# Phase parts of an S4D and GLU kernel stored as blocks of 14 rows, each phase tile loaded by two transfers

## The chip, the cores and the metric

The kernel runs on one NeuronCore of a Trainium2 chip. The metric is the device time of one execution in microseconds (us), of which the median of several runs counts. Beside the times there is one profiled execution of the kernel, with a record of each instruction and transfer.

The engines are named as in the profile: PE is TensorE (its weight loads are PEld), DVE is VectorE, ACT is ScalarE, POOL is GpSimd, and SP is the engine that here only issues transfers. ACT and POOL issue transfers of their own as well. Each engine takes its instructions in a fixed order; an instruction that waits holds all that stand behind it on the same engine.

## The reference

The input x (2048 tokens, 448 channels) is normalised over its channels. Two branches take the result: a state space convolution (S4D) whose kernel of length 2048 is the sum of 256 complex exponentials per channel, applied by FFT, and a gated MLP (GLU) of width 1792. The output is the sum of x and both branches.

```python
def _A_ref(u, log_A_real, A_imag, C_real, C_imag, log_dt, D_skip):
    dt = jnp.exp(log_dt)
    A = -jnp.exp(log_A_real) + 1j * A_imag
    C = (C_real + 1j * C_imag) * dt[:, None]
    P = jnp.exp((A * dt[:, None])[:, :, None] * pos[None, None, :])
    K = 2.0 * jnp.einsum("dn,dnl->dl", C, P).real
    ...
    y = jnp.fft.irfft(Uf * Kf[None, :, :], L2)[:, :, :L]
    return y + u * D_skip[None, None, :]

def _B_ref(x, w_gate, w_up, w_down):
    g = jnp.einsum("bsd,df->bsf", x, w_gate)
    u = jnp.einsum("bsd,df->bsf", x, w_up)
    return jnp.einsum("bsf,fd->bsd", _sigmoid(g) * u, w_down)

xn = _layernorm(x, axis=-1)
return x + _A_ref(xn, ...) + _B_ref(xn, ...)
```

## The kernel before

Two Python generators, conv for the S4D branch and glu for the GLU branch, yield in turns, and a table of weights decides which goes next. So the program text interleaves the two. A scheduler with a cost model of its own then sets the order on each engine from that text, from priorities (hp) and from hints that one instruction is to be issued after another (issue_after). A small edit can so shift many rows.

The GLU works in float32 split into a high and a low part: gate (L693) makes three products per weight tile and x tile into the PSUM tile gu, then ACT's th (L701), DVE's hf (L704), ACT's hh (L709) and DVE's hl (L711). The down products po (L806) collect into acc by DVE (L811). gu and po share four PSUM buffers. Weights are loaded by SP into one buffer, wraw (w_load, L626 and L628, six transfers), then cast into wh by ACT (L743), with the rest in wl by DVE (L747). The second weight of all is loaded into raw1 at the start and cast as wh_268. In the first half of the GLU most weight parts are also stored to memory for later (wt_d L750, dt_d L773).

The S4D branch has four stages. First x is normalised and transposed, and its spectrum's first step is taken (x_spec). Second, prep computes for two halves h of 224 channels the magnitudes and the phases of the exponentials. Each phase has three values, U, V and T, and each is split into a high part (L388, ACT) and a low part (L393, POOL); these six parts per channel are stored to ph_d in memory by SP (L389, L394), one transfer of 112 partitions by 2 by 256 numbers for a part and a half, twelve in all. Third, kgen goes over 56 steps of 8 channels: PE turns the stored parts into angles by a product with a table sel (tr, L526), ACT makes sines and cosines S (L532 to L535), POOL makes powers of the magnitudes me and mf (L504), DVE multiplies both into Et and Ft (L586 to L588), and PE's ko (L600) sums over the states. Fourth, spectra multiplies spectra and transforms back (sp L888, pv L915).

A phase tile ph0 or ph1 holds 16 channels, two sets of eight. Partitions 32g to 32g+11 hold six parts of two channels; 32g+12 and 32g+13 hold ones; 32g+14 to 32g+25 hold the same twelve rows again, which sel multiplies with the other sign. The ones meet a large constant in sel, plus and minus, so that the sum is rounded to whole turns between. phase_load (L470 to L476) fills a tile by eight transfers of 12 partitions, four groups g at two places; the ones are set once by POOL (L468). The tiles are used in turn, and a tile is loaded anew as soon as PE has read it the second time, two tiles ahead:

```python
def phase_load(b):
    t = pht[b % 2]
    src = ph_d[16 * b : 16 * b + 16].rearrange("(k g e) i n -> g (e i) k n", k=2, g=4)
    for at in (0, 14):
        for g in range(4):
            r0 = 32 * g + at
            nc.sync.dma_start(t[r0 : r0 + 12].bitcast(F32), src[g])
```

Of the kernel before, what the change touches and what calls it, by code (L numbers as in the profile page):

```python
# [11 lines left out]
F32 = mybir.dt.float32  # L12
# [8 lines left out]
D = 448  # L21
N = 256
# [5 lines left out]
MAGIC = 1.5 * 2.0**23  # L28
# [27 lines left out]
def _tables():  # L56
# [15 lines left out]
    b = np.arange(NB)[:, None]  # L72
# [36 lines left out]
    for e in range(DC):  # L109
        g, r = e // 2, 6 * (e % 2)  # L110
        for at, sg in ((r, 1.0), (r + 14, -1.0)):
            sel[g, at : at + 2, 0, e] = sg * st
            sel[g, at + 2 : at + 4, 1, e] = sg * st
            sel[g, at + 4 : at + 6, 1, e] = sg
        sel[g, 12, :, e] = MAGIC
        sel[g, 13, :, e] = -MAGIC
    f = lambda v, s: np.ascontiguousarray(v.reshape(s).astype(np.float32))
# [7 lines left out]
        "c_sel": f(sel, (128, 512)),  # L125
        "c_id": np.eye(128, dtype=np.float32),
    }


@with_exitstack  # L130
def s4d_glu_kernel(ctx, tc, io):
    nc = tc.nc
# [7 lines left out]
    acc_d = dram.tile([128, 8, D], F32, name="acc_d")  # L140
    ph_d = dram.tile([D, 6, N], F32, name="ph_d")
    x1_d = dram.tile([64, NB, D], F32, name="x1_d")
# [193 lines left out]
    def prep(pool, h, srcs):  # L336
# [47 lines left out]
        rows = ph_d[2 * CP * h : 2 * CP * h + 2 * CP].rearrange("(t p) i n -> p t i n", t=2)  # L384

        def high(i, src):
            hi = slots[f"P{i}"][:, h]
            nc.scalar.copy(hi, src)  # L388
            nc.sync.dma_start(rows[:, :, 2 * i], three(hi).bitcast(F32))  # L389

        def low(i, src):
            lo = src.bitcast(F32R)
            nc.gpsimd.tensor_tensor(lo, src, slots[f"P{i}"][:, h], ALU.subtract)  # L393
            nc.sync.dma_start(rows[:, :, 2 * i + 1], three(lo).bitcast(F32))  # L394

# [49 lines left out]
    def kgen(pk):  # L445
# [24 lines left out]
        def phase_load(b):  # L470
            t = pht[b % 2]
            src = ph_d[16 * b : 16 * b + 16].rearrange("(k g e) i n -> g (e i) k n", k=2, g=4)
            for at in (0, 14):
                for g in range(4):
                    r0 = 32 * g + at
                    nc.sync.dma_start(t[r0 : r0 + 12].bitcast(F32), src[g])  # L476

# [528 lines left out]
    def conv():  # L1006
        with tc.tile_pool(name="psk", bufs=1, space=PSUM) as ps_, tc.tile_pool(
# [9 lines left out]
            with tc.tile_pool(name="pst", bufs=1, side="right", reuse_waits="tile") as pst:  # L1017
# [33 lines left out]
                nc.gpsimd.tensor_copy(sel[:, 0:1], zs[:, 7:8])  # L1051
                nc.gpsimd.dma_start(sel, io["c_sel"])
                nc.sync.dma_start(wk, io["c_wk"])
                nc.sync.dma_start(wx, io["c_wx"])
# [88 lines left out]
```

## Time and profile before

| quantity | value |
| --- | --- |
| median of 3 runs | 740.25 us (738.54 to 742.46) |
| the profiled execution's own time | 735.94 us |
| its span, first to last instruction | 734.2 us |
| mean granted TensorE clock | 0.978 of full speed |
| bytes moved by the DMA engines | 117.24 MB, mean 160 GB/s |
| SP's transfers (q1) | 91.87 MB, 45.3% of 16 engines' span |
| POOL's transfers (q0) | 5.90 MB, 3.0% of 16 engines' span |

A row of the timeline has its start in us, its length in us, engine, line, operation and what it writes and reads; in brackets stands the idle time ahead of it and what ended that. A row of the chain has start, length and what the chain went through there. A row of waits has in total the us, the times and the longest. PE stands for the matrix products as recorded; their ends are modelled.

### The profile page before, as it was taken

The numbers are of one execution on the slowest core, as the hardware profiler recorded it, in microseconds if no ns is written. First come the engines' busy times: TensorE is split into PE (matmuls) and PEld (weight loads), VectorE is DVE, ScalarE is ACT, GpSimd is POOL, SyncE is SP. The second block draws the span as 40 slices with busy tenths as digits, with TensorE's granted clock in tenths as the row PEclk, the third lists the DMA queues.
The fourth block names the chain that finished last, engine by engine and source line by source line (L and its number), as shares of the span: only waits on it lengthen the run. The fifth ranks groups of instructions, "written<-read, shape, count | busy, mean of one in ns | idle before, by whom it ended". The sixth has DMA issues, their size and how long they took to land.

```text
span 734.2 us, 19242 instructions
## 1 busy us (share of the span) xinstructions
PE 682.4 (93%) x7780; PEld 532.7 (73%) x7780; DVE 557.0 (76%) x776; ACT 421.1 (57%) x650; POOL 355.9 (48%) x423
## 2 busy tenths in 40 slices
PE   2898998999999899999999999998999999999995
PEld 2666787877877687565888877887877778776784
DVE  5899995699978989768667987977975555565543
ACT  3646483578677868797487787677652222323320
POOL 2110055684975986548467498486855001441002
PEclk9999999999999999699999999999999999999998
DMA  9946445444324635345972332332158999999845
GB/s 208 225 131 179 113 135 176 134 138 168 96 89 135 221 86 155 98 127 174 278 191 88 111 108 80 100 104 80 45 163 272 257 253 241 266 262 221 199 118 160
DMA packets 102984, 117.24 MB, mean 160 GB/s; under 512 B 13232, under 2 KB 90864, under 8 KB 102896
## 3 DMA queue, kind: packets, MB, share of 16 engines
q1 hardware_dynamic: 78736, 91.87, 45.3%
q10 hardware_dynamic: 21584, 18.24, 9.6%
q0 software_dynamic: 2576, 5.90, 3.0%
q8 instruction: 61, 1.00, 0.6%
q14 instruction: 27, 0.22, 0.1%
HBM read 72.13 MB, written 43.84 MB: 158 GB/s over the span
## 4 chain that ended last, share of the span: by engine, by line
PE 55%; DVE 17%; ACT 8%; DMA 8%; issue 5%; POOL 4%; SPq 2%; ACTq 1%; DVEq 0%; POOLq 0%
PE gu L693 23%; PE po L806 13%; PE sp L888 5%; PE ko L600 5%; PE pv L915 3%; PE tr L526 3%; DVE Ft L588 2%; DVE Et L587 2%; ACT S L535 2%; DVE Et L586 2%; DVE pm L440 2%; ACT S L532 1%; DMA sx<-x_d 1%; ACT S L533 1%; DMA tb<-in_c_tab_dram 1%
## 5 line engine op out<-in xcount | busy, mean ns | idle before, releaser
L504 POOL TENSOR_TENSOR me<-me,pm 128x32 f32<-128x32 f32 (+1 forms) x168 | 137.5, 819 | 114.8 <-DVE Et L587 102.9
L504 POOL TENSOR_TENSOR mf<-mf,pm 128x64 f32<-128x64 f32 (+1 forms) x112 | 113.8, 1016 | 5.2
L693 PE MATMUL gu<-xh,wh 128*128 128x512 f32 x336 | 100.2, 404 | 2.6 <-DVE acc L811 1.1
L693 PE MATMUL gu<-xh,wl 128*128 128x512 f32 x336 | 97.8, 396 | 0.0
L693 PE MATMUL gu<-xl,wh 128*128 128x512 f32 x336 | 96.2, 394 | 0.0
L586 DVE TENSOR_TENSOR Et<-me,S 128x1024 f32<-128x1024 f32 x56 | 80.1, 1430 | 18.1 <-ACT S L535 17.0
L587 DVE TENSOR_TENSOR Et<-me,S 128x1024 f32<-128x1024 f32 x56 | 78.9, 1410 | 15.4 <-ACT me L517 12.0
L806 PE MATMUL po<-dh,hh 128*128 128x448 f32 x224 | 85.1, 380 | 3.7 <-DVE acc L811 3.0
L588 DVE TENSOR_TENSOR Ft<-mf,S 128x1024 f32<-128x1024 f32 x56 | 79.3, 1416 | 5.5 <-ACT S L535 4.5
L806 PE MATMUL po<-dl,hh 128*128 128x448 f32 x224 | 83.2, 371 | 0.0
L806 PE MATMUL po<-dh,hl 128*128 128x448 f32 x224 | 82.4, 369 | 0.0
L693 PEld LDWEIGHTS gu<-xh,wh 128*128 128x128 f32 x336 | 61.2, 190 | 23.5 <-issue 6.1
L600 PEld LDWEIGHTS ko<-Et,Ft 128*32 128x32 f32 x3584 | 54.5, 111 | 32.3 <-DVE Ft L588 13.8
L532 ACT ACTIVATE S<-tr 128x1024 f32<-128x1024 f32 x56 | 57.7, 1030 | 33.2 <-PE tr L526 31.5
L600 PE MATMUL ko<-Et,Ft 128*32 128x64 f32 x3584 | 64.9, 223 | 12.4 <-DVE Ft L588 12.4
L693 PEld LDWEIGHTS gu<-xh,wl 128*128 128x128 f32 x336 | 63.7, 190 | 14.7 <-DVE ys L257 0.7
L693 PEld LDWEIGHTS gu<-xl,wh 128*128 128x128 f32 x336 | 63.8, 190 | 14.3 <-issue 0.7
L709 ACT CAST hh<-hf 128x512 fp32r<-128x512 f32 x56 | 34.9, 623 | 62.7 <-DVE hf L704 62.6
L704 DVE SCALAR_TENSOR_TENSOR hf<-th,gu 128x512 f32<-128x512 f32 x56 | 38.2, 682 | 40.4 <-PE gu L693 34.7
L701 ACT ACTIVATE th<-gu 128x512 f32<-128x512 f32 x56 | 33.6, 601 | 59.6 <-PE gu L693 46.1
L535 ACT ACTIVATE S<-S,hpi 128x1024 f32<-128x1024 f32 x56 | 65.6, 1172 | 0.0
L811 DVE SCALAR_TENSOR_TENSOR acc<-po,acc 128x448 f32<-128x448 f32 x80 | 48.1, 617 | 19.4 <-PE po L806 19.4
(198 smaller groups left out, 1295.1 us busy)
## 6 DMA issues: line engine op xcount, KB each, us to landing
sk_d<-sk ACTq DMA_DIRECT2D x14, 512.0 KB
sx<-x_d SPq DMA_DIRECT2D x32, 224.0 KB
skl<-sk_d SPq DMA_DIRECT2D x16, 448.0 KB
vp<-v_d SPq DMA_DIRECT2D x16, 448.0 KB
v_d<-vt SPq DMA_DIRECT2D x62, 112.0 KB
ph<-ph_d SPq DMA_DIRECT2D x224, 24.0 KB
wt_d<-wh SPq DMA_DIRECT2D x9, 512.0 KB
wt_d<-wl SPq DMA_DIRECT2D x9, 512.0 KB
```

Source lines behind the costliest of these rows:

```text
L504: ins = nc.gpsimd.tensor_tensor(m[:, :, w + a : 2 * w : n], m[:, :, a:w:n], par(base + i).unsqueeze(2).to_broadcast([128, 4 * DC, w // n]) ...
L532: nc.scalar.activation(rows(cs), pv, AF.Abs)
L535: sins[:] = [nc.scalar.activation(cs, cs, AF.Sin, scale=-TWO_PI, bias=hpi)]
L586: v.tensor_tensor(Et[:, :, :, 32:64], two(me[:, :, 32:64]), S[:, 1::-1], ALU.mult)
L587: v.tensor_tensor(Et[:, :, :, 0:32], two(me[:, :, 0:32]), S[:, 1:3, :, ::-1], ALU.mult)
L588: fts[:] = [v.tensor_tensor(Ft, two(mf), S[:, 3:5], ALU.mult)]
L600: mm = nc.tensor.matmul(ko[32 * j : 32 * j + 32, sl], Ft[:, cc, DC * h + 4 * q + j], Et[:, cc, DC * h + 4 * q + j], start=(k == 0), stop=( ...
L693: glu_mm[:] = [nc.tensor.matmul(ps, a_, b_, start=(n == 0), stop=(n == len(mm) - 1))]
L704: marks[1] = v.scalar_tensor_tensor(hf, th, 1.0, pgu[1], ALU.add, ALU.mult)
L806: glu_mm[:] = [nc.tensor.matmul(po, a_[:, bs], w_, start=(n == 0), stop=(n == 3 * fc - 1))]
L811: v.scalar_tensor_tensor(acc[:, b], po, 0.5, acc[:, b], ALU.mult, ALU.add)
L888: mm = nc.tensor.matmul(to, tb[:kk, t, 64 * c : 64 * c + 64], rhs, start=True, stop=True, skip_group_check=True,)
```

## The change

In memory each channel now has a block of 14 rows: six parts, two rows of ones, and the six parts again. So four channels are 56 rows that follow each other both in memory and in the tile, and a tile is loaded by two transfers of 56 partitions, at partitions 4 to 59 and 68 to 123. sel has its rows moved to match. Every part is stored twice (store, 24 transfers for 12), and the ones are copied into ph_d once from a new constant input, by POOL's queue. Line numbers move by two to six.

```diff
     for e in range(DC):
-        g, r = e // 2, 6 * (e % 2)
-        for at, sg in ((r, 1.0), (r + 14, -1.0)):
+        g = e // 2
+        r = 4 * (1 - g % 2) + 14 * (e % 2)
+        for at, sg in ((r, 1.0), (r + 8, -1.0)):
             sel[g, at : at + 2, 0, e] = sg * st
             sel[g, at + 2 : at + 4, 1, e] = sg * st
             sel[g, at + 4 : at + 6, 1, e] = sg
-        sel[g, 12, :, e] = MAGIC
-        sel[g, 13, :, e] = -MAGIC
+        sel[g, r + 6, :, e] = MAGIC
+        sel[g, r + 7, :, e] = -MAGIC
...
+        "c_one": np.ones((D, 2, N), np.float32),
...
-    ph_d = dram.tile([D, 6, N], F32, name="ph_d")
+    ph_d = dram.tile([D, 14, N], F32, name="ph_d")
...
+        def store(i, src):
+            for at in (i, i + 8):
+                nc.sync.dma_start(rows[:, :, at], src)
+
         def high(i, src):
             hi = slots[f"P{i}"][:, h]
             nc.scalar.copy(hi, src)
-            nc.sync.dma_start(rows[:, :, 2 * i], three(hi).bitcast(F32))
+            store(2 * i, three(hi).bitcast(F32))
 
         def low(i, src):
             lo = src.bitcast(F32R)
             nc.gpsimd.tensor_tensor(lo, src, slots[f"P{i}"][:, h], ALU.subtract)
-            nc.sync.dma_start(rows[:, :, 2 * i + 1], three(lo).bitcast(F32))
+            store(2 * i + 1, three(lo).bitcast(F32))
...
         def phase_load(b):
             t = pht[b % 2]
-            src = ph_d[16 * b : 16 * b + 16].rearrange("(k g e) i n -> g (e i) k n", k=2, g=4)
-            for at in (0, 14):
-                for g in range(4):
-                    r0 = 32 * g + at
-                    nc.sync.dma_start(t[r0 : r0 + 12].bitcast(F32), src[g])
+            src = ph_d[16 * b : 16 * b + 16].rearrange("(k g e) i n -> g (e i) k n", k=2, g=2)
+            for g in range(2):
+                nc.sync.dma_start(t[64 * g + 4 : 64 * g + 60].bitcast(F32), src[g])
...
                 nc.gpsimd.dma_start(sel, io["c_sel"])
+                nc.gpsimd.dma_start(ph_d[:, 6:8], io["c_one"])
```

The scheduler gives all engines another order in the first half; on PE the later rows, from about the middle of the list, stand as before. Three places matter here. The first is ACT at the start: xh and xr are the casts of the transposed x, wh_268 the cast of the second raw weight. Before:

```order
L743 CAST wh_228<-wraw_128 128x1024
L272 ACTIVATE xn0_117<-acc_100,zs_80,ys_79 128x448 x2
L221 CAST xh_94<-tr_200 128x512
L221 CAST xh_94<-ko_201 128x512
L221 CAST xh_94<-kp_202 128x512
L224 CAST xr_96<-gu_203 64x512
L743 CAST wh_268<-raw1_114 128x1024
```

With the change:

```order
L747 CAST wh_228<-wraw_128 128x1024
L274 ACTIVATE xn0_117<-acc_100,zs_80,ys_79 128x448 x2
L747 CAST wh_268<-raw1_114 128x1024
L223 CAST xh_94<-tr_200 128x512
L223 CAST xh_94<-ko_201 128x512
L223 CAST xh_94<-kp_202 128x512
```

The cast of the second weight has moved ahead of all casts of x.

The second place is SP's queue around the end of prep: ph_d<- are the stores (p01, P2 the high parts, w3 and others the low), wraw the next weight's load, rd a row of the down weight, ph0<- the first phase load. Before:

```order
L389 DMA ph_d_58<-p01_375 112x2x256
L626 DMA wraw_1300<-in_B_w_gate_dram 128x3x128
...
L394 DMA ph_d_58<-w3_380 112x2x256
L389 DMA ph_d_58<-P2_115 112x2x256
L750 DMA wt_d_61<-wl_1307 128x1024
L394 DMA ph_d_58<-w3_392 112x2x256
L626 DMA wraw_1456<-in_B_w_gate_dram 128x3x128
L628 DMA wraw_1456<-in_B_w_gate_dram 64x128 x2
...
L634 DMA rd_1536<-in_B_w_down_dram 128x448
L476 DMA ph0_1095<-ph_d_58 12x2x256 x8
```

With the change:

```order
L390 DMA ph_d_58<-p01_376 112x2x256 x6
...
L390 DMA ph_d_58<-fr_396 112x2x256 x2
L390 DMA ph_d_58<-w3_393 112x2x256 x2
L630 DMA wraw_1301<-in_B_w_gate_dram 128x3x128
L632 DMA wraw_1301<-in_B_w_gate_dram 64x128 x2
L630 DMA wraw_1301<-in_B_w_up_dram 128x3x128
L632 DMA wraw_1301<-in_B_w_up_dram 64x128 x2
L638 DMA rd_1346<-in_B_w_down_dram 128x448
L480 DMA ph0_1108<-ph_d_58 56x2x256 x2
L480 DMA ph1_1109<-ph_d_58 56x2x256 x2
```

The weight that was issued second among the stores (wraw_1300) is now behind all of them (wraw_1301), and one weight fewer is loaded ahead of the first phase tile.

The third place is PE at the first tr. gu_1191 before and gu_1192 with the change are the last gate product of the same weight group, after which 72 po products follow. Before, tr stands among the po of the second x tile:

```order
L806 MATMUL po_1255<-dl_880,hh_945 128x448
L806 MATMUL po_1255<-dh_877,hl_946 128x448
L806 MATMUL po_1255<-dh_1018,hh_1052 128x448
L526 MATMUL tr_1143<-sel_74,ph0_1095 128x512 x2
L806 MATMUL po_1255<-dl_1021,hh_1052 128x448
```

With the change:

```order
L697 MATMUL gu_1192<-xr_99,wl_1077 128x512
L697 MATMUL gu_1192<-xl_98,wh_1069 128x512
L530 MATMUL tr_1144<-sel_74,ph0_1108 128x512 x2
L697 MATMUL gu_1192<-xl_98,wh_1069 128x512 x2
L810 MATMUL po_1212<-dh_878,hh_874 128x448
```

The first tr has moved ahead by 40 po products and two of gu, so that all 72 po stand behind it.

## The prediction

> **What bounds the kernel now.** I read the totals of the page first, then the chain of waits, then busy time by stage, then who waited for the instructions that the change touches.
>
> ```profile
> span 734.2 us, 19242 instructions
> PE 682.4 (93%) x7780; PEld 532.7 (73%) x7780; DVE 557.0 (76%) x776; ACT 421.1 (57%) x650; POOL 355.9 (48%) x423
> PE 55%; DVE 17%; ACT 8%; DMA 8%; issue 5%; POOL 4%; SPq 2%; ACTq 1%; DVEq 0%; POOLq 0%
> ```
>
> TensorE (PE) is busy for 682.4 of 734.2 us and holds 55% of the chain; SP's queue holds 2%. The change takes no matrix product away, so it can only alter the 51.8 us in which PE stands still. These lie as follows (columns: stage, its length, busy us of PE, PEld, DVE, ACT, POOL, then granted clock, DMA share, GB/s):
>
> ```profile
> 0.00:19.00 19.00, 5.88 (x24) 4.43 (x25) 11.53 (x36) 6.61 (x9) 3.83 (x17) 1.00 0.95 210
> 19.00:115.60 96.60, 89.86 (x428) 68.32 (x427) 91.43 (x169) 55.98 (x96) 22.54 (x20) 0.96 0.62 160
> 115.60:136.00 20.40, 17.44 (x79) 15.52 (x78) 11.66 (x20) 7.62 (x10) 10.46 (x20) 0.92 0.57 175
> 136.00:360.00 224.00, 209.45 (x2905) 158.53 (x2904) 188.84 (x205) 167.38 (x252) 155.92 (x175) 0.96 0.45 137
> 360.00:560.00 200.00, 195.38 (x3006) 160.26 (x3005) 162.92 (x171) 140.01 (x201) 133.05 (x156) 1.00 0.40 119
> 560.00:734.20 174.20, 164.40 (x1347) 125.61 (x1346) 90.59 (x178) 43.52 (x83) 30.12 (x37) 0.99 0.91 227
> ```
>
> PE's idle time is 13.1 us in the start, 6.7 to 115.6 us, 3.0 around the first phase tile, 14.6 to 360 us, 4.6 to 560 us and 9.8 in the tail. In the start the DMA engines are full (share 0.95); from 136 to 560 us, where nearly all phase loads lie, they are under half busy. From 19 to 115.6 us VectorE is busy for 91.4 of 96.6 us: a delay that enters there is not made up.
>
> **The change part by part.** First the removed loads. 224 issues become 56.
>
> ```profile
> L476 SPq DMA_DIRECT2D ph<-ph_d x224: 290/365/1562, 121.0 to 512.9; - x112
> who waited for it (us, times):
>   DVE wl L747: 6.5, 1
>   ACT wh L743: 0.7, 1
>   PE tr L526: 0.2, 1
> ```
>
> 168 issues of 0.365 us are 61 us of SP's time, spread over 392 us. But PE waited once for a phase tile, 0.2 us, and the largest row, VectorE's 6.5 us, falls at 117 to 123.7 us, where it stood for a weight load whose own issue came before the first phase load (below). So the 61 us are hidden by PE's own work. I take -0.2 us; the bounds are 0 and -1, the rows of PE and ACT together. Each pair of loads moves 224 KB in place of 192 KB, 0.9 MB more over the stage; the DMA share of 0.40 to 0.45 there covers it.
>
> Second, the ones: 448 x 2 x 256 floats, 0.92 MB, copied from one place of memory to another. The order puts this transfer on POOL's queue right behind the identity, ahead of the four loads of dm, which stood at 2.10 us. It then runs beside the loads on which the first products wait. Rows of the start (the chain's landing of the second raw weight; ACT's casts; PE's first products; the nearest transfer on POOL's queue, with its us from issue to landing):
>
> ```profile
> 2.10 2.13 POOL L1057 DMA_DIRECT2D dm<-in_A_D_skip_dram  x4
> 12.61 3.68 DMA raw<-in_B_w_up_dram
> 15.50 0.58 ACT L221 CAST xh<-tr 128x512 fp32r<-128x512 f32 x1 [1.76 <-PE tr L212]
> 15.98 0.59 ACT L221 CAST xh<-ko 128x512 fp32r<-128x512 f32 x1
> 17.41 1.05 ACT L743 CAST wh<-raw 128x1024 fp32r<-128x1024 f32 x1
> 16.14 1.72 PE L693 MATMUL gu<-xh,wh 128*128 128x512 f32 x6
> 18.52 0.98 PE L693 MATMUL gu<-xh,wh 128*128 128x512 f32 x3 [0.66 <-ACT wh L743]
> sel<-in_c_sel_dram POOLq DMA_DIRECT2D x1, 256.0 KB, 10.5
> 121.86 1.85 DMA ph<-ph_d
> ```
>
> At the stage's 210 GB/s the copy is worth 0.92 / 0.210 = 4.4 us if all of it goes ahead of the raw weight; that is the upper bound, and 0 the lower. The nearest row is sel: 256 KB on the same queue beside a full SP queue, 10.5 us; less the 1.85 us that a phase load takes to land, that is 262 KB in 8.65 us, 30 GB/s. From about 4 us until the raw weight lands at 16.3 us the copy would move 0.37 MB, which costs the others 1.8 us. I take 2.0 us.
>
> The Trainium skill (DMA: Bandwidth & Descriptors, section "Queues, rings and completion order") says that each DMA engine takes turns between the queue rows that have work, a packet at a time. By equal turns the copy would have half the engines and all of it would pass before the raw weight: 4.4 us and a time 2.4 us above mine. The sel row, 30 of some 210 GB/s, agrees with turns but not with equal ones.
>
> The scheduler has also moved ACT's cast of that weight (wh_268) ahead of the casts of x, for which every first product waits. So the first product starts after landing, wh, and one xh: 16.3 + 2.0 + 1.05 + 0.5 = 19.9 us in place of 16.14; the pause of 0.66 us at 18.52 goes. That is +3.1 us, with +1.1 and +5.5 as bounds. VectorE's full stage behind it keeps the loss.
>
> Third, the stores: 24 for 12, 2.75 MB more, and what is queued behind them on SP. In the order all 24 now stand ahead of the load of wraw_1301, where before its equal, wraw_1300, was issued at 98 us among them.
>
> ```profile
> SPq L389 <- ACT p L388: 8.3, 1, 8.3
> 114.35 1.21 SPq L394 DMA_DIRECT2D ph_d<-w  x1
> 115.61 1.05 SPq L626 DMA_DIRECT2D wraw<-in_B_w_gate_dram  x1
> 120.38 0.53 SPq L634 DMA_DIRECT2D rd<-in_B_w_down_dram  x1
> 121.00 6.83 SPq L476 DMA_DIRECT2D ph<-ph_d  x16
> 99.29 2.82 POOL L393 TENSOR_TENSOR aim<-aim,p 112x512 fp32r<-112x512 f32 x1 [10.63 <-PE gu L693]
> 114.06 1.20 POOL L770 TENSOR_TENSOR dl<-rd,dh 128x448 fp32r<-128x448 f32 x1
> 114.64 0.84 PE L693 MATMUL gu<-xl,wh 128*128 128x512 f32 x3
> 125.74 0.74 PE L806 MATMUL po<-dh,hh 128*128 128x448 f32 x1 [2.96 <-DVE acc L811]
> 80.00:121.00 41.00, 40.10 (x194) 33.19 (x186) 35.24 (x57) 19.27 (x38) 18.94 (x16) 1.00 0.52 154
> ```
>
> SP waited 8.3 us ahead of its first store, so twelve more issues of about 0.4 us fit into its waits for ACT and POOL. The last stores cannot go before POOL has made the last low part. Its six subtractions and one dl fill 99.3 to 114.1 us now; without the stretched ones (2.82 and 3.50 where 1.6 to 1.75 is the rule) they would end near 110. So the last store is issued between 111 and 116 us. From there it is the same distance as now: 4.8 us for the six weight issues, 0.6 for rd, two phase issues of 6.83 / 16 = 0.43, and 1.85 to land, 8.1 us. The first phase tile is there at 119 to 124 us. PE now reaches the place of the change's first tr, before the last two products of gu_1192, at about 115 us, which was no matter when tr stood 40 rows later. VectorE's order has the preparation ahead of hf, which frees PSUM, so PE will be 1 to 3 us late there itself (it has 0.9 us to spare from 80 to 121 us). The new stall is 1 to 8 us, 4.5 as the middle. Queued behind tr on PE are all products of po; ACT's S and VectorE's Et wait for tr. The old stall of 2.96 us, VectorE held by the weight load behind the stores, goes, but VectorE now stands in the same way at wl_1308, and Et, Ft come ahead of two of the acc that free PSUM. I put 1.5 us for that and for the late hf. Sum 4.5 - 2.96 + 1.5 = +3.0 us, with -2 and +7 as bounds; these hold the stores' own traffic too (2.75 MB at 160 to 210 GB/s beside a share of 0.52 leaves next to nothing free from 98 to 116 us).
>
> Sum: 3.1 + 3.0 - 0.2 = +5.9 us, against the profiled execution's 735.94 us (span 734.2 and 1.74 around it): 741.8. The median of the runs shown, 740.25, lies 4.3 us above that execution, so I put 740.25 + 5.9 = **746 us**. The bounds together give -1.9 to +12.5, 738 to 753 us, the forecast's own range.
>
> **The rivals.** *Everything is hidden.* The copy stays behind the weights and the earlier tr just meets its tile: +1.1 for the cast's place, -2 at the opening, 739 us. For it: PE did without the SP queue until now. Against: the start has a DMA share of 0.95, and the cast's place alone holds PE.
>
> *Faster.* The preparation ends earlier, SP is free 5 us sooner (12 issues of 0.43) and the phase work gets ahead of TensorE's order. Then PE stops waiting for Ft:
>
> ```profile
> PE ko L600 <- DVE Ft L588: 9.6, 9, 2.3
> ```
>
> This is from 121 to 360 us. If these 9.6 us and the 2.96 us go while the start costs 3.1 and the first tr 1.5, the sum is -8 us, 732 us. It decides where the first tile lands before PE gets there, at 115 to 118 us. Against it: the order moves tr and ko of the first half forward as well, by some rows each, so PE asks earlier too; and Ft is VectorE's, 189 of 224 us busy there.
>
> *Slower than forecast.* The forward place of ko meets an unchanged Ft, and the 9.6 us double: 746 + 9.6 = 756 us. For it: the second half's order is the same as before, so nothing later gives it back. Against it: a PE that starts late waits less.
>
> **How the numbers follow.** Forecast 0.52, hidden 0.20, faster 0.18, more 0.10. About 0.5%, 3.7 us, is what this kernel's measurement can tell from no change. Above 744 us: 0.45 of the forecast, 0.03 of the hidden case and the 0.10, 0.58. Below 736.5 us: 0.16 and 0.02, 0.18. Between: 0.24. The range 734 to 756 us leaves out part of the faster case and the end of the last.
>
> **What would show it.** In the profile after: the first gu product near 20 us in place of 16.1, with ACT's wh ahead of xh and its wait on the raw weight; the stage to 19 us with 3 us less PE work; the first tr idle for some us with the phase load as its releaser; wl of the next weight behind the stores on SP; 56 phase issues and no new wait for a phase tile after 140 us. I am wrong if the first product is still at 16 to 17 us, if the first tr does not wait, or if PE's idle time from 136 to 360 us moves by more than 4 us from 14.6.

## The result and the profile after

| | before | with the change |
| --- | --- | --- |
| median of 7 runs | 738.54 us (736.31 to 742.46) | 746.41 us (743.89 to 748.81) |
| ratio | 1 | 1.0099, 95% interval 1.0073 to 1.0125 |
| the profiled execution's own time | 735.94 us | 746.06 us |
| PE busy | 682.4 us | 683.3 us |

The change costs 7.9 us by the medians. A ratio, here and below, leaves out the executions recorded as slow (over 1.5% above the fastest of their kernel, one each of runs 3 and 11), and it is not quite the quotient of the medians. The two profiled executions lie 10.1 us apart, so some 2 us of what follows is the chance of two single executions. First the page's totals:

```profile
span 744.3 us, 19031 instructions
PE 683.3 (92%) x7780; PEld 534.2 (72%) x7780; DVE 558.5 (75%) x776; ACT 420.5 (57%) x650; POOL 365.1 (49%) x424
```

PE has the same work and stands still for 61.0 us in place of 51.8. Where, the same stages as in the prediction show (length, busy us of PE, PEld, DVE, ACT, POOL, granted clock, DMA share, GB/s):

```profile
0.00:19.00 19.00, 3.94 (x16) 2.96 (x16) 8.13 (x26) 4.28 (x5) 4.46 (x18) 1.00 0.93 229
19.00:115.60 96.60, 85.77 (x387) 63.67 (x387) 89.94 (x169) 51.55 (x88) 16.58 (x16) 0.93 0.62 165
115.60:136.00 20.40, 17.41 (x82) 14.51 (x81) 11.00 (x21) 12.51 (x23) 10.89 (x20) 1.00 0.78 241
136.00:360.00 224.00, 206.83 (x2826) 159.58 (x2824) 187.13 (x204) 161.13 (x241) 158.33 (x167) 0.96 0.44 137
360.00:560.00 200.00, 195.43 (x3075) 161.36 (x3072) 166.56 (x173) 145.38 (x210) 139.14 (x159) 1.00 0.41 123
560.00:744.30 184.30, 173.94 (x1405) 132.14 (x1403) 95.74 (x188) 45.70 (x87) 35.67 (x45) 0.99 0.89 224
```

Length less PE busy, against before: 15.1 us in the start (13.1), 10.8 to 115.6 us (6.7), 3.0 in the opening (3.0), 17.2 to 360 us (14.6), 4.6 to 560 us (4.6), 10.4 in the tail (9.8).

The start, in the timeline, with the copy's row of the DMA issues (KB, then us from issue to landing):

```profile
2.10 0.65 POOL L1057 DMA_DIRECT2D ph_d<-in_c_one_dram  x1
12.60 1.28 ACT L747 ACT_TABLE_LOAD   x1 [12.60 <-DMA wraw<-in_B_w_up_dram]
18.37 1.04 ACT L747 CAST wh<-raw 128x1024 fp32r<-128x1024 f32 x1 [2.12 <-DMA raw<-in_B_w_up_dram]
19.95 3.83 PE L697 MATMUL gu<-xh,wh 128*128 128x512 f32 x9 [1.48 <-ACT xh L223]
```

```profile
ph_d<-in_c_one_dram POOLq DMA_DIRECT2D x1, 896.0 KB, 7.5
```

The first weight is there at 12.60 us (before 10.08), the second at 18.37 (before 12.61 + 3.68 = 16.29), and the first gate product starts at 19.95 (before 16.14).

The opening of the phase stage, on SP and PE, and who waited for the phase loads:

```profile
117.70 0.41 PE L432 MATMUL ko<-ident,a 112*128 112x112 f32 x2 [1.72 <-ACT GG L434]
118.77 1.42 SPq L390 DMA_DIRECT2D ph_d<-w  x2
...
125.01 1.68 SPq L480 DMA_DIRECT2D ph<-ph_d  x4
128.49 0.70 PE L530 MATMUL tr<-sel,ph 128*128 128x512 f32 x2 [1.27 <-DMA ph<-ph_d]
```

```profile
L480 SPq DMA_DIRECT2D ph<-ph_d x56: 307/386/1222, 125.0 to 518.6; - x56
who waited for it (us, times):
  ACT wh L747: 3.6, 1
  DVE wl L751: 2.5, 1
  PE tr L530: 1.3, 1
```

The stores end and the first phase load goes 4.0 us later than before (121.00), but PE is some 12 us late itself, so it waits 1.27 us only, and never again for a phase tile. With the wait of 1.72 us for GG (a copy by ACT in prep) that is the whole idle time of the opening.

**A marker of how late a kernel runs.** After every fourth step of kgen ACT copies the spectrum's first products out of PSUM (sk from kp), 14 times in all. The fourth and the seventh of these copies, first before, then with the change:

```profile
277.88 0.63 ACT L556 COPY sk<-kp 128x512 f32<-128x512 f32 x1
...
379.06 0.62 ACT L556 COPY sk<-kp 128x512 f32<-128x512 f32 x1 [1.09 <-PE kq L550]
```

```profile
283.07 0.64 ACT L560 COPY sk<-kp 128x512 f32<-128x512 f32 x1
...
388.77 0.63 ACT L560 COPY sk<-kp 128x512 f32<-128x512 f32 x1 [0.52 <-PE kq L554]
```

The changed kernel is 8.9 us late at the first of the 14 copies (188.4 us before), 5.2 at the fourth, 9.7 at the seventh, and between 8.8 and 9.7 at all that follow. So part of the lateness is made up on the way, then a new one enters between 280 and 380 us, and from there to the last of these copies, at 549 us before, it hardly changes. Between the seventh and the last copy the rows of PE and ACT stand in the same order in all the kernels below, but for a few. The first 12 to 14 us of lateness, at 115 us, are not what is seen at the end. The experiments follow this.

### The profile page after: what moved, and what is told of

It reads as the page before. It is cut to its first block, busy times and chain, and to the rows that moved or that the text cites. A ratio compares the mean times of both kernels' runs of the same rounds, so it can differ in the third digit from the quotient of the medians.

```text
span 744.3 us, 19031 instructions
## 1 busy us (share of the span) xinstructions
PE 683.3 (92%) x7780; PEld 534.2 (72%) x7780; DVE 558.5 (75%) x776; ACT 420.5 (57%) x650; POOL 365.1 (49%) x424
## 4 chain that ended last, share of the span: by engine, by line
PE 50%; DVE 17%; DMA 11%; ACT 9%; issue 5%; POOL 4%; SPq 2%; ACTq 1%; POOLq 0%; DVEq 0%
PE gu L697 18%; PE po L810 13%; PE sp L892 6%; PE ko L604 5%; PE pv L919 3%; PE tr L530 3%; DVE Et L590 2%; DVE Et L591 2%; DMA sx<-x_d 2%; DVE Ft L592 2%; POOL me L508 2%; ACT S L539 1%; POOL mf L508 1%; ACT S L536 1%; DMA xe<-in_A_u_dram 1%
## 5 line engine op out<-in xcount | busy, mean ns | idle before, releaser
L508 POOL TENSOR_TENSOR me<-me,pm 128x32 f32<-128x32 f32 (+1 forms) x168 | 144.3, 859 | 103.1 <-DVE Et L591 92.7
L508 POOL TENSOR_TENSOR mf<-mf,pm 128x64 f32<-128x64 f32 (+1 forms) x112 | 119.8, 1070 | 4.6
L590 DVE TENSOR_TENSOR Et<-me,S 128x1024 f32<-128x1024 f32 x56 | 82.9, 1480 | 26.6 <-ACT S L539 21.7
L591 DVE TENSOR_TENSOR Et<-me,S 128x1024 f32<-128x1024 f32 x56 | 78.1, 1395 | 14.4 <-ACT me L521 11.8
L604 PEld LDWEIGHTS ko<-Et,Ft 128*32 128x32 f32 x3584 | 55.2, 112 | 34.8 <-issue 12.7
L697 PEld LDWEIGHTS gu<-xh,wh 128*128 128x128 f32 x336 | 62.7, 194 | 22.6 <-issue 4.9
L604 PE MATMUL ko<-Et,Ft 128*32 128x64 f32 x3584 | 66.1, 224 | 13.7 <-DVE Ft L592 11.9
L697 PEld LDWEIGHTS gu<-xl,wh 128*128 128x128 f32 x336 | 64.0, 191 | 14.4 <-issue 0.7
```

The source lines that it names most:

```text
L508: ins = nc.gpsimd.tensor_tensor(m[:, :, w + a : 2 * w : n], m[:, :, a:w:n], par(base + i).unsqueeze(2).to_broadcast([128, 4 * DC, w // n]) ...
L590: v.tensor_tensor(Et[:, :, :, 32:64], two(me[:, :, 32:64]), S[:, 1::-1], ALU.mult)
L591: v.tensor_tensor(Et[:, :, :, 0:32], two(me[:, :, 0:32]), S[:, 1:3, :, ::-1], ALU.mult)
L604: mm = nc.tensor.matmul(ko[32 * j : 32 * j + 32, sl], Ft[:, cc, DC * h + 4 * q + j], Et[:, cc, DC * h + 4 * q + j], start=(k == 0), stop=( ...
L697: glu_mm[:] = [nc.tensor.matmul(ps, a_, b_, start=(n == 0), stop=(n == len(mm) - 1))]
```

## The experiments

Theory A is that of the prediction: the copy in the start and the cast order that comes with it make the start late, and the rest keeps it. B: the 24 stores and the opening are the loss. C: any new order costs. D was formed after the first four runs: the order of the rows of 285 to 345 us keeps the loss. Each run is timed against the kernel before on the same chip.

**1. The copy alone.**

```diff
+        "c_one": np.ones((D, 2, N), np.float32),
...
+    sp_d = dram.tile([D, 2, N], F32, name="sp_d")
...
                 nc.gpsimd.dma_start(sel, io["c_sel"])
+                nc.gpsimd.dma_start(sp_d, io["c_one"])
```

> The kernel before, with nothing changed but that the 0.92 MB of ones are copied at the start, by POOL's queue, into a place of memory that nobody reads. The scheduler answers by the same order of ACT as in the changed kernel (wh_268 ahead of xh). Theory A (the loss is the start's copy with the cast order that it brings, and what the DVE-full stage makes of it): first gu product at 19.5 to 20.5 us in place of 16.1, PE 8 to 12 us late at 86 us, and a time of 744 to 748 us. Theory B (the loss comes from the 24 stores and the opening of the phase stage): the start shifts, but the time is 738 to 741 us. Theory C (the loss is the price of any new order, whatever it is): 740 to 748, with PE's late places elsewhere than in the changed kernel.

738.7 us, ratio 0.9994 (0.9964 to 1.0023). The start is as late as A says: the first gate product at 19.51 us, and PE some 12 us behind at 86 us, by the GLU's products. The time is that of the kernel before. So this late start, with the order that this run has after it, costs nothing in the end, and A in this form is wrong.

**2. The cast put back.**

```diff
+                acts.append(mv.ins)
...
+                            second = len(raws) == 1
...
-                            with hp(HP):
+                            with hp(HP), tc.issue_after(acts[0]) if second else nullcontext():
                                 nc.scalar.copy(wh, raw)
...
```

> The changed kernel with one hint more: the cast of the second weight (wh_268) is issued behind the casts of x, as before. The copy stays in the start. Theory A in two halves. If the copy's traffic costs (weights land 2.0 to 2.5 us later): first gu product at 18 to 18.6 us, xn on ACT still at 14.8, time 743 to 746 us. If the place of the cast costs: first gu product at 16.1 to 16.9 us and a time of 738 to 741 us. Theory B (stores and opening): 745 to 747 us whatever the start does.

746.53 us, ratio 1.0087 (1.0056 to 1.0118). This is the number that B gave. The first gate product stands at 19.06 us, later than either half of A said, 0.9 us earlier than with the change, though this execution's first weight landed 0.55 us later (13.15 us). So of the 3.8 us by which that product is late, the cast's place is 1 to 1.5 us and the copy's traffic the rest. On the time neither shows.

**3. The copy late.** The ones are copied behind a small store that waits for the scales zs.

```diff
-                nc.gpsimd.dma_start(ph_d[:, 6:8], io["c_one"])
...
                 x_scales(sm, 8, 8)
+                nc.gpsimd.dma_start(ph_d[0:128, 6, 0:1], zs[:, 15:16])
+                nc.gpsimd.dma_start(ph_d[:, 6:8], io["c_one"])
```

> The changed kernel with the copy of the ones held until the last normalisation's scales are there (a small store of them into the place of the ones is written over by the copy), so that it stands on POOL's queue ahead of the first low part, at some 80 to 95 us. Stores, sel and two-transfer loads as in the changed kernel. The order of all engines up to there is then that of the kernel before (ACT's rows are the same to the 100th). Theory A: first gu product at 16.1 to 16.9 us, PE within 1 us of the kernel before at 86 us, and the opening's loss alone is left, 0 to +3 us: 738 to 742 us. Theory B (stores and opening): 744 to 748 us. If the copy costs wherever it stands, weight loads between 85 and 115 us land late and the time is 742 to 746.

738.05 us, ratio 0.996 (0.993 to 0.999). First gate product at 16.03 us. With the stores, the blocks of 14 rows, sel and the two-transfer loads all in place, the loss is gone, and B falls. It is A's number, but run 1 has taken A's reason away. What this run has besides the early start is the order of the kernel before, but for a few dozen rows. It keeps all that the change does to the loads, and is the fastest form of it: faster than the changed kernel by 1.4%, and by its ratio at least as fast as the one before.

**4. Two loads alone.**

```diff
...
-            src = ph_d[16 * b : 16 * b + 16].rearrange("(k g e) i n -> g (e i) k n", k=2, g=4)
-            for at in (0, 14):
-                for g in range(4):
-                    r0 = 32 * g + at
-                    nc.sync.dma_start(t[r0 : r0 + 12].bitcast(F32), src[g])
+            src = ph_d[16 * b : 16 * b + 16].rearrange("(k e) i n -> (e i) k n", k=2)
+            for r0 in (0, 64):
+                nc.sync.dma_start(t[r0 : r0 + 48].bitcast(F32), src)
```

(The lines left out move the rows of sel to match.)

> The kernel before with two transfers for a phase tile and nothing else: 48 rows of parts of eight channels, which already follow each other in memory, go to partitions 0 to 47 and the same 48 again to 64 to 111; the ones are the tile's own at 48 and 49, and sel has its rows moved to match. No copy, twelve stores as before. The parts of a channel now lie in more than one group of 32 partitions. My term T0 (the removed issues are hidden, -0.2 us, 0 to -1): 737 to 739.5 us, no wait of PE for a phase tile. Rival (SP freed of 61 us brings weights and tiles earlier and PE's 9.6 us of waits for Ft and 2.96 us of the opening go): 727 to 734 us. If the new order costs by itself: above 741 us.

741.37 us, ratio 1.0024 (0.9993 to 1.0054): no gain from 168 issues fewer, if anything a small loss. PE waits for no phase tile. But from 300 to 345 us PE stands still for 9.5 us, where the kernel before has 2.2, and in the very places where the changed kernel waits (the longest, 3.46 us, for the same xl). That led to theory D. PE's waits from 285 to 345 us of the changed kernel (in brackets the idle time and what ended it):

```profile
293.99 0.44 PE L214 MATMUL gu<-ident,xt 128*128 128x128 f32 x2 [1.21 <-DVE hf L708]
298.36 1.10 PE L604 MATMUL ko<-Et,Ft 128*32 128x64 f32 x64 [1.64 <-DVE Ft L592]
304.42 0.74 PE L530 MATMUL tr<-sel,ph 128*128 128x512 f32 x2 [0.90 <-ACT S L538]
309.65 1.03 PE L530 MATMUL tr<-sel,ph 128*128 128x512 f32 x2 [1.36 <-ACT S L538]
311.97 1.94 PE L604 MATMUL ko<-Et,Ft 128*32 128x64 f32 x64 [1.29 <-DVE Et L590]
323.81 0.64 PE L214 MATMUL gu<-ident,xt 128*64 128x128 f32 x2 [3.26 <-DVE xl L224]
335.00 0.96 PE L697 MATMUL gu<-xh,wh 128*128 128x512 f32 x3 [0.65 <-ACT x L679]
```

They sum to 10.3 us.

**5. Eight loads of 14 partitions.** The changed kernel, with its tile loaded in eight pieces.

```diff
-                nc.sync.dma_start(t[64 * g + 4 : 64 * g + 60].bitcast(F32), src[g])
+                for e in range(4):
+                    r0 = 64 * g + 4 + 14 * e
+                    nc.sync.dma_start(t[r0 : r0 + 14].bitcast(F32), src[g, 14 * e : 14 * e + 14])
```

> The changed kernel with each phase tile loaded by eight transfers of 14 partitions in place of two of 56; the copy in the start, the 24 stores, the blocks of 14 rows and sel stay as in the changed kernel. Same bytes. The scheduler's order is that of the changed kernel up to some 280 us, but from there to the end of the phase stage it is, row for row on PE, DVE and ACT, that of the run with the copy alone (e1_copy_alone, 738.7 us). Theory D (the loss is the order of the rows of 285 to 345 us, where the changed kernel's PE waits 10 us against 4 before, with the late start's lateness not regained): 737 to 741 us, though every part of the change but the count of loads is there. Theory B (24 stores and late tiles behind them, with a late start): 744 to 748 us. If the lateness of 12 to 14 us at 115 us stays for another reason: 744 to 748 as well.

740.82 us, ratio 1.0041 (1.0016 to 1.0065). More issues, the same bytes, the same late start and stores, and more than half of the loss is gone. PE's rows to 280 us are nearly those of the changed kernel, the later ones are those of run 1. PE's waits from 285 to 345 us here:

```profile
297.74 0.77 PE L606 MATMUL ko<-Et,Ft 128*32 128x64 f32 x40 [1.26 <-DVE Ft L594]
299.60 0.41 PE L214 MATMUL gu<-ident,xt 128*64 128x128 f32 x2 [1.10 <-DVE xl L224]
304.06 1.10 PE L606 MATMUL ko<-Et,Ft 128*32 128x64 f32 x64 [0.46 <-DVE Ft L594]
326.06 0.44 PE L214 MATMUL gu<-ident,xt 128*128 128x128 f32 x2 [0.22 <-ACT x L681]
```

They sum to 3.0 us. What differs is seen best at the longest wait. A block of xt is transposed in two parts, six transposes (128x128) and then two (64 rows), which need the PSUM tile that DVE's xl of the first part frees. PE with the change, then in this run from the last two of the six on (rows between left out):

```profile
318.14 0.87 PE L214 MATMUL gu<-ident,xt 128*128 128x128 f32 x6
...
320.03 0.52 PE L604 MATMUL ko<-Et,Ft 128*32 128x64 f32 x18
323.81 0.64 PE L214 MATMUL gu<-ident,xt 128*64 128x128 f32 x2 [3.26 <-DVE xl L224]
```

```profile
311.24 0.44 PE L214 MATMUL gu<-ident,xt 128*128 128x128 f32 x2
311.61 0.86 PE L606 MATMUL ko<-Et,Ft 128*32 128x64 f32 x44
...
316.55 0.98 PE L283 MATMUL gu<-xt,wx 32*64 32x448 f32 x8
317.46 0.41 PE L606 MATMUL ko<-Et,Ft 128*32 128x64 f32 x10
317.81 0.41 PE L214 MATMUL gu<-ident,xt 128*64 128x128 f32 x2
```

In run 5 there are 6 us of other products between the two parts. In the changed kernel there are 1.5 us of kp, kq and ko, and xl comes late, because DVE has Et, Et, hf and xt ahead of it and Et waits for POOL:

```profile
318.50 1.32 DVE L591 TENSOR_TENSOR Et<-me,S 128x1024 f32<-128x1024 f32 x1 [1.75 <-POOL me L508]
...
321.32 0.67 DVE L708 SCALAR_TENSOR_TENSOR hf<-th,gu 128x512 f32<-128x512 f32 x1
...
323.35 0.41 DVE L224 TENSOR_TENSOR xl<-gu,xh 128x256 fp32r<-128x256 f32 x1
```

**6. Four loads.**

```diff
-                nc.sync.dma_start(t[64 * g + 4 : 64 * g + 60].bitcast(F32), src[g])
+                for k in range(2):
+                    nc.sync.dma_start(t[64 * g + 4 : 64 * g + 60, k].bitcast(F32), src[g, :, k])
```

> The changed kernel with each phase tile loaded by four transfers of 56 partitions, one for each set of eight channels, in place of two that hold both sets. Same bytes. The order of PE, DVE and ACT is that of the changed kernel but for some ten rows, the late part of the phase stage included. Theory D (the order of 285 to 345 us): 744.5 to 748 us, with the same waits of PE at 285 to 345 us (about 10 us). If instead the two large transfers cost by themselves (they land late or hold others up): 738 to 742 us.

746.82 us, ratio 1.0121 (1.0093 to 1.0148). The order stays that of the changed kernel, and so does the loss; PE stands still for 9.6 us from 280 to 345 us. Runs 5 and 6 both split the loads of the same kernel and were timed together: the loss follows the order.

**7. The stores doubled alone.**

```diff
+        def store(i, src):
+            for to in (rows, rows2):
+                nc.sync.dma_start(to[:, :, i], src)
...
-            src = ph_d[16 * b : 16 * b + 16].rearrange("(k g e) i n -> g (e i) k n", k=2, g=4)
-            for at in (0, 14):
+            srcs = [p[16 * b : 16 * b + 16].rearrange("(k g e) i n -> g (e i) k n", k=2, g=4) for p in (ph_d, p2_d)]
+            for at, src in zip((0, 14), srcs):
```

> The kernel before with each phase part stored twice, the second time into another place of memory, from which the second half of each tile is loaded: 24 stores, 224 loads of 12 partitions, no copy of ones. The rows of ACT and DVE in the start and of PE from 280 us are those of the kernel before; between, the order differs. My term of the third part without the late start (new stall at the first tr less the old stall of 2.96 us): 738 to 743 us with a wait for the first phase tile of 1 to 5 us. Theory D: 737.5 to 741 us whatever the opening does. Theory B (the stores are the loss): 744 to 748 us.

745.66 us, ratio 1.0097 (1.007 to 1.0124). This is B's number, and D's was wrong. But B's reason isn't there either. On SP and PE:

```profile
121.69 1.58 SPq L483 DMA_DIRECT2D ph<-ph_d  x4
```

```profile
127.18 0.62 PE L533 MATMUL tr<-sel,ph 128*128 128x512 f32 x2
...
189.74 1.08 PE L533 MATMUL tr<-sel,ph 128*128 128x512 f32 x2 [4.37 <-ACT S L541]
```

With 24 stores the first phase load goes 0.7 us later than before, PE's first tr does not wait, and PE stands still for 0.7 us from 116 to 140 us, where before it was 3.0. The loss lies from 140 to 280 us: 18.5 us of idle time in place of 9.8. By the trace over 300 of PE's rows stand elsewhere than before, all but a few between 140 and 380 us and about half of them behind 280 us; so the expectation was wrong that the rows from 280 us are those of the kernel before. In the longest wait ACT has the cast of a weight ahead of the S that tr needs, and the weight lands late:

```profile
186.31 1.04 ACT L750 CAST wh<-wraw 128x1024 fp32r<-128x1024 f32 x1 [2.87 <-DMA wraw<-in_B_w_up_dram]
```

So the order of rows seems to cost again, but in another stretch: D was too narrow about the place. This is read from the longest wait alone; no run tried it.

**8. The copy by ACT.**

```diff
-                nc.gpsimd.dma_start(ph_d[:, 6:8], io["c_one"])
+                nc.scalar.dma_start(ph_d[0:128, 6, 0:1], zs[:, 7:8])
+                nc.scalar.dma_start(ph_d[:, 6:8], io["c_one"])
```

> The changed kernel with the copy of the ones issued by ACT after the first normalisation's scales (a small store of them into the place of the ones is written over). The start's order on ACT and DVE is a third one, neither that of before nor that of the changed kernel; from there to the end of the phase stage it is, but for two rows, that of the changed kernel, the rows of 285 to 345 us included. Theory D: 743 to 748 us even if the start is a few us less late, with PE's waits of 10 us at 285 to 345 us. Theory A (the start's lateness sets the time): the time follows the start, 738 to 742 us if the first gu product is back at 16 to 17 us and PE is within 4 us of the kernel before at 86 us.

744.12 us, ratio 1.0089 (1.0056 to 1.0122). The first gate product is back at 16.09 us, and the time is that of the changed kernel, whose order this run shares but for its first part. PE is some 9 us behind at 86 us all the same, by 12.4 us of idle time from 19 to 116 us.

**9. Half the copy in the start.** Run 3 with its copy cut in two; the small store ahead of it stays.

```diff
-                nc.gpsimd.dma_start(ph_d[:, 6:8], io["c_one"])
+                for i in range(2):
+                    nc.gpsimd.dma_start(ph_d[:, 6 + i], io["c_one"][:, i])
```

> The run with the late copy (e3_copy_late, 738.05 us) with the copy cut in two, 0.46 MB each: one row of ones is copied in the start, the other late. Nothing else differs in the program, but the scheduler's order from some 140 us to the end of the phase stage is, but for two rows, that of the changed kernel in place of that of the kernel before. Theory D (the order of the rows of 285 to 345 us keeps the loss): PE idle for 7 to 10 us from 300 to 345 us in place of 2.9, and a time of 743 to 747 us. Theory A (the start's lateness, by the copy's bytes, sets the time): half of the changed kernel's loss, 740 to 742.5 us.

745.03 us, ratio 1.008 (1.0054 to 1.0107). One half is copied at 2.1 us, the other at 99. One transfer cut in two turns run 3 nearly into the changed kernel: half the bytes in the start, most of the loss, 6.9 us of idle time from 300 to 345 us.

**10 and 11. Half and a quarter of the copy alone.** Run 1 with fewer bytes.

```diff
-                nc.gpsimd.dma_start(sp_d, io["c_one"])
+                nc.gpsimd.dma_start(sp_d[:224], io["c_one"][:224])
```

(and with 112 in the second.)

> The run with the copy alone (e1_copy_alone, 738.7 us) with half of the copy's bytes, 0.46 MB into a place that nobody reads. Phase loads, stores and sel are those of the kernel before. The order from some 140 us on is that of e1_copy_alone. Theory D: PE idle for 0.5 to 1 us from 300 to 345 us, and 735 to 739 us. If the copy's bytes in the start cost by themselves: 739 to 742 us.

736.39 us, ratio 0.997 (0.9942 to 0.9998), with PE idle for 2.1 us from 300 to 345 us, a little more than expected. With run 1, bytes copied in the start cost nothing in the end.

> The same with a quarter of the copy, 0.23 MB. The casts of the start stand as before, the order up to some 280 us is otherwise near that of e1_copy_alone, and from there to the end of the phase stage it is a new one, neither that of before nor of the changed kernel. Work and transfers are those of the kernel before but for 0.23 MB. Theory D: the time is set by PE's idle time up to 345 us and nothing else: 738.5 us and 0.8 us for each us of it over the 36.7 us of the kernel before, within 2 us; it may so come out anywhere from 735 to 746. A theory by bytes, stores or loads: 738 to 740 us.

742.51 us, ratio 1.0029 (0.9998 to 1.006). Fewer bytes than in run 10, and slower rather than faster. Theory D's rule, from 39.2 us of idle time up to 345 us against 36.8, gives 738.5 + 0.8 x 2.4 = 740.4: its sign, and 2.1 us short of the median, just outside its bound. This run has the lowest granted clock of all from 300 to 345 us, 0.77, which the rule leaves out.

**12. New places, eight loads.** Run 4 with its loads cut into eight.

```diff
-                nc.sync.dma_start(t[r0 : r0 + 48].bitcast(F32), src)
+                for e in range(4):
+                    nc.sync.dma_start(t[r0 + 12 * e : r0 + 12 * e + 12].bitcast(F32), src[12 * e : 12 * e + 12])
```

> The run with two loads alone (e4_two_loads_alone, 741.4 us) with its phase tile loaded by eight transfers of 12 partitions; the parts' places in the tile and sel are those of that run. PE, DVE and ACT have row for row the order of the kernel before. Theory D: 737.5 to 740 us, with PE idle for about 2 us from 300 to 345 us in place of 9.5; the 1.9 us of e4_two_loads_alone were its order. If the new places of the parts cost PE or the transfers something: 741 us or more.

Ratio 0.9998 (0.9969 to 1.0026), median 740.4 us, just above what D gave. With the order of the kernel before it keeps that kernel's pace: all 14 copies of sk within 0.6 us of it but one (2.1). Its idle time from 300 to 345 us is 5.2 us, not the 2 expected, with a higher granted clock (0.96 against 0.89), so the one may stand in for the other. By the ratio the places of the parts cost nothing.

**All runs together.** PE's idle time in five stages (length less PE's busy time of the windows), the lag of the fourth and the seventh copy of sk behind the kernel before, and the ratio. "Order" says whose rows PE and ACT follow through the phase stage.

| run | order | 0-19 | 19-116 | 116-140 | 140-280 | 280-345 | lag 4th | lag 7th | ratio |
| --- | --- | --- | --- | --- | --- | --- | --- | --- | --- |
| before | before | 13.1 | 6.8 | 3.0 | 9.8 | 4.2 | 0 | 0 | 1 |
| 3 copy late | near before | 12.3 | 6.9 | 2.1 | 7.5 | 8.2 | -4.5 | -1.4 | 0.996 |
| 12 new places | before | 13.3 | 6.9 | 2.5 | 9.8 | 7.7 | -2.1 | -0.4 | 0.9998 |
| 1 copy alone | run 1 | 15.2 | 9.7 | 0.1 | 6.0 | 3.2 | 2.0 | 0.5 | 0.9994 |
| 5 eight loads | run 1 from 280 us | 15.8 | 11.3 | 0.7 | 5.8 | 3.3 | 3.4 | 1.1 | 1.0041 |
| 10 half copy alone | run 1 | 14.7 | 9.4 | 0.2 | 6.2 | 4.9 | 0.9 | -0.7 | 0.997 |
| the change | the change | 15.1 | 10.8 | 3.8 | 5.6 | 10.3 | 5.2 | 9.7 | 1.0099 |
| 2 cast back | the change | 15.1 | 12.4 | 1.8 | 9.2 | 9.8 | 6.6 | 9.0 | 1.0087 |
| 6 four loads | the change | 15.3 | 12.5 | 2.4 | 6.7 | 9.6 | 4.8 | 8.6 | 1.0121 |
| 8 copy by ACT | the change | 12.7 | 12.4 | 1.6 | 5.6 | 11.5 | -0.7 | 4.9 | 1.0089 |
| 9 half in start | the change | 14.4 | 9.3 | 2.5 | 6.5 | 9.7 | 4.4 | 6.5 | 1.008 |
| 4 two loads | partly the change | 12.2 | 7.9 | 3.5 | 5.8 | 12.7 | -3.7 | 4.1 | 1.0024 |
| 7 stores doubled | its own | 13.1 | 6.8 | 0.7 | 18.5 | 6.2 | 8.4 | 6.5 | 1.0097 |
| 11 quarter copy | its own from 280 us | 12.9 | 13.0 | 0.7 | 6.6 | 6.2 | 0.1 | 6.9 | 1.0029 |

The five kernels with the changed kernel's order lie between 1.008 and 1.012, whatever their loads, copies and start are. The six with the order of before or of run 1 lie between 0.996 and 1.004. The stage from 280 to 345 us doesn't set the time by itself, though. The same rows leave 4.2 us of idle time in the kernel before and 7.7 in run 12. And run 4 has the most, 12.7 us, with a ratio of 1.0024 only: its start isn't late and it comes to that stage 3.7 us ahead. The rule that theory D gave for run 11, 738.5 us and 0.8 us for each us of idle time up to 345 us over 36.8 us (the sum of a row's five stages), lies within 2.2 us of the median of every kernel in the table; it counts the stages alike, and so says nothing of one stage against another. The stage from 280 to 345 us of the kernel before, the changed one and run 5:

```profile
280.00:345.00 65.00, 60.84 (x790) 38.99 (x788) 52.80 (x63) 52.51 (x86) 40.95 (x51) 0.89 0.48 140
```

```profile
280.00:345.00 65.00, 54.67 (x814) 38.12 (x805) 48.08 (x54) 49.12 (x80) 39.88 (x47) 0.89 0.42 125
```

```profile
280.00:345.00 65.00, 61.68 (x858) 40.52 (x857) 56.88 (x64) 54.15 (x89) 43.01 (x49) 0.95 0.54 155
```

PE works 54.67 us of these 65 with the change and 61.68 in run 5, at clocks of 0.89 and 0.95. The two kernels are as late as each other where this stage begins, within 1.8 us (fourth copy), and 8.6 us apart at the seventh copy. By the ratios they are 0.6% apart, 4.3 us; run 6, timed together with run 5, is 0.8% or 5.9 us behind it.

What stays open: run 5 keeps 3 us of the loss, and nothing here says from what. No run changed the order of rows and nothing else, since the scheduler sets it from the program. Runs 5 and 6 differ by eight loads against four, and the early part differs between run 3 and run 9. That larger loads cost by themselves is excluded by run 3, which has two per tile and no loss; that they cost only in a late start was not tried apart from the order. The profiled executions of runs 1 and 10 were among their slowest (742.24 and 740.78 us), 6.3 and 4.8 us longer than that of the kernel before, though their last copy of sk is at most 0.9 us late: some 5 us came in behind it. Lags are of one execution each, and repeats of a kernel spread by 4 us to either side, so differences of 2 or 3 us in the table mean little.

## Why the prediction was right in its number

Forecast 746 us, measured 746.41. The number fits better than the reasons, and in part by chance: the forecast was +5.9 us on 740.25, and what came was +7.9 us on 738.54.

**The removed loads, -0.2 us.** As a direct cost this is right: 56 issues, one wait of 1.3 us at the first tr, none for a phase tile later; run 4 gains nothing from it. What failed is the step that took this edit for done with that. Two loads or eight for a tile moves the scheduler's rows between 280 and 380 us (run 5), as the place of the copy does (run 9 against run 3), and that order is, as far as the runs show, the larger part of the loss: 5.2 us of lag before it and 9.7 after, where run 5 goes from 3.4 to 1.1. The prediction read the order at the start, at SP's queue and at the first tr, and took the rest of the phase stage's idle time as given.

**The start, +3.1 us.** Its steps held one by one: the second weight 2.1 us later (2.0 said), the first gate product at 19.95 us (19.9 said), the pause behind it gone. PE's work to 19 us fell by 1.9 us, not 3. The copy ran at 0.92 MB in 7.5 us, 122 GB/s, four times the 30 GB/s that I took from sel's row; the weights still lost only 2 to 2.5 us. While it ran, from 2.1 to 9.6 us, the engines moved 297 GB/s, so its share was 0.41. The Trainium skill (DMA: Bandwidth & Descriptors, "Queues, rings and completion order") has the engines take turns between queues, and the copy's share is nearer to equal turns than the 30 of 210 that I took; the weights' delay is still under the 4.4 us that I had worked out from that rule. What was wrong is the sentence after the sum, that VectorE's full stage keeps the loss. To 115 us it keeps it, and adds to it: the GLU's products are 4.4 us late at 51 us, 10 at 86 and 12 at 112. After that it is regained: in run 1 the first copy of sk is 6.5 us late, the fourth 2.0, the seventh 0.5. PE's idle time from 116 to 280 us shows it, 12.8 us before and 6.1 in run 1. Part of this may be that a PE that comes late finds Et, Ft and S ready. Part may be the new order: run 4, whose start isn't late, has 5.8 us from 140 to 280 us in place of 9.8, with nearly the changed kernel's rows there.

**The stores and the opening, +3.0 us.** Nothing of it came. The opening's idle time is the same 3.0 us: the first tr waits 1.27 us (4.5 said), 1.72 us for GG are new, and the old stall of 2.96 us is gone. The phase load was issued 4.0 us later, but the sum had PE come to its place 1 to 3 us late, and it came some 12 us late. In run 7, where PE isn't late, 24 stores leave it less idle than before, and the phase load goes only 0.7 us later: there SP's new issues fell into its waits for ACT and POOL, as the prediction itself said when it costed them.

**The sum** was then right by two errors that cancel: +6.1 us for start and opening that do not last, and 0 for the rows of 280 to 380 us, where PE's idle time to 345 us alone grew by 6.1 us. That they are of one size is luck.

**The rivals.** "Everything is hidden" has run 3's number (738.05 us, 739 said), but in another way: there the copy isn't in the start. "Faster" needed the waits for Ft to go: over the whole trace they are 11.9 us against 12.4. "Slower" named the right stage for a loss and the wrong wait: Ft didn't double; the waits for xl, S, Et and hf are what grew from 285 to 345 us.

**The test that I set** was met and said little: the idle time from 136 to 360 us moved by 2.6 us, less than the 4 named. Inside, 140 to 280 us gave back 4.2 us and 280 to 345 us lost 6.1.

## What to carry to other kernels

Where a scheduler sets the order, the price of an edit can be that of the order that it brings, over the whole program: compare the rows to the end, and look in the trace at each stretch that moved, not only where the edited instructions stand. An early delay can be regained later, as in run 1, so follow one row that recurs through the program, and see where its lag last changes. A control that keeps every edit but splits one transfer differently helps to tell the edit from its order.

## What the runs showed that I had not expected

A short idle time of PE can cost more than itself. Around 66 to 70 us the changed kernel's PE waits 1.02 and 1.83 us, and the granted clock stands at half from 68 to 76 us (first PE's rows, then two of the stretches of 2 us, with the clock third from the end):

```profile
66.03 0.98 PE L283 MATMUL tr<-xn,wx 32*64 32x448 f32 x8 [1.02 <-ACT x1ab L294]
68.84 0.74 PE L810 MATMUL po<-dh,hh 128*128 128x448 f32 x1 [1.83 <-DVE hf L708]
```

```profile
68.00:70.00 2.00, 1.16 (x3) 1.08 (x4) 2.00 (x6) 1.93 (x4) 0.00 (x0) 0.50 0.94 290
...
74.00:76.00 2.00, 2.00 (x7) 1.78 (x6) 1.48 (x2) 1.98 (x3) 0.00 (x0) 0.50 0.14 35
```

From 60 to 80 us the mean clock is 0.74, which is 20 x 0.26 = 5.2 us of full speed lost, more than the 2.85 us of the waits. Before, two waits of about 0.7 and 1.0 us at the same place cost one shorter dip, 0.91 and 1.8 us:

```profile
60.00:80.00 20.00, 17.59 (x93) 12.64 (x89) 20.00 (x39) 16.64 (x25) 0.00 (x0) 0.91 0.58 156
```

These are three steps and one step of about 1.7 us. The Trainium skill (TensorE: Matmul & The Clock Gate, "What's actually happening") has the clock at half after an idle window of about 3.4 us, which by estimate would be 1.7 us lost for each window. The size of the steps agrees with that; that PE has to be idle for 3.4 us does not, since its longest wait here was 1.83 us. The 3.4 us (5.2 less 1.8) between the two dips could be the larger part of the 5.7 us that the GLU's products fall back from 51 to 86 us; no run tried it. It is not the loss that stays: the mean granted clock up to 345 us is 0.96 in both kernels, since the kernel before has more of its dips later.
